# A linear-attention and feed-forward kernel: the opening's instructions in another order

## The chip, the cores and the metric

The kernel runs on one core of a Trainium2 chip. A core has five engines with queues of their own: TensorE (PE in the profile; its weight loads are PEld), VectorE (DVE), ScalarE (ACT), GpSimd (POOL) and SyncE (SP), which here only issues transfers. Sixteen DMA engines move data between the chip's large memory and the on-chip buffers. Matrix products land in PSUM, eight banks of 128 partitions by 512 fp32 numbers.

The metric is the device time of one execution in microseconds (us). The kernel before takes 286.4 us, the median of three runs (285.63, 286.40 and 286.46).

## The reference, cut to what matters

```python
batch, n_heads, seq, head_dim = (8, 8, 576, 64)
def phi(x):
    return np.where(x > 0, x, np.exp(x) - 1.0) + 1.0
q_p, k_p = (phi(q), phi(k))
kv = np.einsum('bhsd,bhse->bhde', k_p, v)
z = np.sum(k_p, axis=2)
num = np.einsum('bhsd,bhde->bhse', q_p, kv)
den = np.einsum('bhsd,bhd->bhs', q_p, z)[..., None] + 1e-06
x = (num / den)            # then heads side by side: 4608 tokens x 512
h = x @ w_in               # 512 x 2048
g = h - np.tanh(h)
out = g @ w_out            # 2048 x 512
```

Inputs and output are fp32; the kernel multiplies in bf16. phi is computed as min(exp(x), max(x, 0) + 1).

## The kernel before, in words

**Stages.** The feed-forward part goes over nine chunks `c` of 512 tokens. In each, layer 1 makes 16 blocks `fi` of 128 hidden columns (four matmuls each, `l1mm`, L418; tanh on ScalarE and the difference on VectorE, `l1act` and `l1act2`), and layer 2 makes four output blocks (`l2mm`, L439). The attention of the next batches is written between these steps by hand: the lists `s1[fi]` and `s2[s]` hold what is issued after a step. TensorE is busy almost without a pause in them. The order of the instructions of each engine is the order in which they are written, and each waits by semaphore counts for what it needs.

**The opening** is what comes before layer 1 of chunk 0: the attention of batch 0 cannot hide behind anything. A batch has 576 tokens and eight heads; heads are taken in four pairs `p`, and the eight heads lie as two halves `i`, two `hg` and two `h`, so that a product over 64 tokens and 64 dimensions uses a quarter of TensorE, and four run as one quad (`quads`). With J = 9 token groups:

1. `load` (L88) brings q, k and v of batch 0 by halves, `load_wi` (L107) w_in by column ranges, then k of batch 1, two parts of w_out, q and v of batch 1 (L91). All go through POOL's queue, which casts fp32 to bf16, in the order written; a load also waits until the eighth load before it has landed.
2. `spin` (L506) multiplies zeros while nothing else is there: 18 matmuls, later 5 and 6.
3. phi of q's halves (Exp L131, max L132, min L133), nine transposes per half on TensorE (`a_qT_pe`, L161), each half copied from two PSUM banks (L165 on ScalarE, L167 on VectorE).
4. phi of k. The second half goes in two parts by `h` (L128 to L130).
5. `b0_z` sums phi(k) over tokens by a matmul with ones, for each half (L247); `b0_zc` masks the sums into `kz` (L251).
6. `b0_kv` multiplies phi(k) and v (L257), `b0_kz` copies the result to `kz` (L261), on VectorE for half 0 and on ScalarE for half 1.
7. `a_den` (L326, L330) makes the denominators in bank 4, VectorE takes the reciprocal (L339).
8. `b0_num` multiplies kv and q of a half (L267) into two banks, `b0_evac` (L287) copies both banks to `ns` by one ScalarE instruction.
9. `b0_spread` spreads the reciprocals to the layout of `num` by fp32 matmuls into banks 4 to 7 (L294), `b0_scale` multiplies (L298): four pairs in the order 0, 2, 1, 3, first for the first 256 tokens, then for the next 256. Pairs 0 and 2 belong to half 0, 1 and 3 to half 1.
10. The first four blocks of layer 1 in chunk 0 (L642) go by 256 tokens and by pair, as the scales come.

Before the change the order on TensorE in steps 5 to 9 is z(0), kv(0), z(1), den, num(0), kv(1), num(1), spread.

**Later places that the prediction names.** In layer 2 of chunk 0, after its eighth step (`s2[7]`), TensorE transposes q of batch 1 (`a_qT_pe`, L161) and multiplies phi(k) and v of batch 1 (`a_kv`, L179). phi of that q is issued at `s2[3]` and `s2[4]` (L131 to L133).

## Time and profile before

| | |
|---|---|
| median of three runs | 286.4 us (285.63 to 286.46) |
| profiled execution | 286.08 us, its span 284.3 us |
| PE busy | 274.7 us, 97% of the span |
| DVE, ACT, POOL busy | 175.7, 146.2, 74.2 us |
| layer 1 matmuls (L418) | 121.8 us |
| layer 2 matmuls (L439) | 122.7 us |
| first matmul of layer 1, chunk 0 (L642) | begins at 16.66 us |
| instruction packets on queue q8 | 16, 0.26 MB |

The span is the time from the first to the last instruction of the profiled execution; its own time is 1.8 us longer. In a line of the timeline the first number is the start, the second the time covered, both in us; then the engine, the line of the kernel, what is written and read with its shape, how many instructions were merged, and in brackets how long the engine was idle before and what ended that. "issue" there means that the profile shows nothing that it waited for. In the chain that ended last each line is a piece of the last chain: start, length, what. A busy PE is not PE at its peak, since the ends of matmuls are modelled. An idle engine off that chain costs nothing. A load has landed when each of the sixteen DMA engines has set its completion mark; the trace has the time of each mark. A few matmul records are missing from a trace.

### The profile page before, as it was taken

Reading aid. Unit: us, or ns where it says so; the run is one execution under the profiler, and the core shown is the slowest. Engines: PE = TensorE matmul, PEld = TensorE weight load, DVE = VectorE, ACT = ScalarE, POOL = GpSimd, SP = SyncE. Lnnn points to the kernel's source line nnn. Section 1 sums busy time; section 2 is a strip of 40 time slices with the busy share of each in tenths; the row PEclk is TensorE's granted clock in tenths of the full one; section 3 lists DMA queues with packets and bytes.
Section 4 is the critical chain, followed back from the end, with each engine's and each line's share of the span. In section 5 each row is a group of like instructions: output and inputs, shape, how many; then the busy total and the mean of one; then the engine's idle time right before and its main releaser. Section 6 shows DMA issues by size and latency. Waiting matters only on the chain.

```text
span 284.3 us, 5076 instructions
## 1 busy us (share of the span) xinstructions
PE 274.7 (97%) x2071; PEld 131.7 (46%) x2099; DVE 175.7 (62%) x278; ACT 146.2 (51%) x178; POOL 74.2 (26%) x66
## 2 busy tenths in 40 slices
PE   8879999999999999999999999999999999999995
PEld 3564464444544454445444544454444444444443
DVE  5849977997479773976397638764770167006600
ACT  4638657847345663666355736672651365125411
POOL 8642030030260536143605360506050000000000
PEclk9999999999999999999999999999999999999999
DMA  6999999998992299038913692241115210230032
GB/s 105 187 206 213 207 206 207 232 167 158 230 234 67 58 198 220 8 85 141 222 36 77 102 233 74 48 108 41 36 24 116 59 34 2 59 80 10 2 74 74
DMA packets 38215, 32.99 MB, mean 116 GB/s; under 512 B 16016, under 2 KB 33840, under 8 KB 38064
## 3 DMA queue, kind: packets, MB, share of 16 engines
q0 software_dynamic: 17488, 18.35, 39.9%
q1 hardware_dynamic: 20544, 14.18, 20.0%
q8 instruction: 16, 0.26, 0.3%
q10 hardware_dynamic: 160, 0.13, 0.1%
q14 instruction: 7, 0.06, 0.1%
HBM read 38.01 MB, written 9.46 MB: 167 GB/s over the span
## 4 chain that ended last, share of the span: by engine, by line
PE 84%; DMA 11%; POOL 2%; issue 1%; DVE 0%; POOLq 0%
PE ps_all L439 40%; PE ps_all L418 39%; DMA v<-in_v_dram 8%; DMA w_in_sb<-in_moe_w_in_dram 3%; PE ps_all L179 2%; PE ps_all L267 1%; PE ps_all L676 1%; POOL v L88 0%; POOL kraw L88 0%; POOL qraw L88 0%; POOL v L473 0%; PE ps_all L275 0%; POOL qraw L91 0%; PE ps_all L330 0%; PE ps_all L161 0%
## 5 line engine op out<-in xcount | busy, mean ns | idle before, releaser
L439 PE MATMUL ps_all<-w_out_sb,gT 128*128 128x512 bf16 x543 | 122.7, 379 | 1.4 <-issue 0.8
L418 PE MATMUL ps_all<-xT,w_in_sb 128*128 128x512 bf16 x549 | 121.8, 379 | 0.7 <-issue 0.2
L425 DVE TENSOR_TENSOR gT<-ps_all,th 128x1024 bf16<-128x1024 f32 x64 | 77.8, 1218 | 47.0 <-ACT th L424 47.0
L424 ACT ACTIVATE th<-ps_all 128x1024 f32<-128x1024 f32 x64 | 65.6, 1024 | 47.7 <-PE ps_all L418 47.0
L418 PEld LDWEIGHTS <-w_in_sb 128*128 128x128 bf16 x560 | 54.6, 98 | 65.6
L439 PEld LDWEIGHTS <-gT 128*128 128x128 bf16 x560 | 53.8, 98 | 63.2 <-issue 0.2
L448 ACT COPY osb<-ps_all 128x512 f32<-128x512 f32 (+1 forms) x36 | 20.9, 583 | 56.6 <-PE ps_all L439 45.3
L238 POOL TENSOR_TENSOR qp<-qp,rd 128x1152 bf16<-128x1152 bf16 x10 | 21.0, 2119 | 39.1 <-issue 23.7
L224 POOL TENSOR_TENSOR pr<-qp,zb 128x1152 f32<-128x1152 bf16 x10 | 23.5, 2363 | 23.9 <-ACT zb L217 21.6
L131 ACT ACTIVATE e<-qraw 128x1152 bf16<-128x1152 bf16 x16 | 18.5, 1161 | 8.3 <-DMA qraw<-in_q_dram 8.3
L229 DVE TENSOR_REDUCE dn<-pr 128x9 f32<-128x576 f32 x20 | 14.5, 746 | 12.2 <-POOL pr L224 12.2
L131 ACT ACTIVATE e<-kraw 128x1152 bf16<-128x1152 bf16 x15 | 17.4, 1161 | 0.0
L133 DVE TENSOR_TENSOR qp<-e,r 128x1152 bf16<-128x1152 bf16 x16 | 12.1, 758 | 5.4 <-ACT e L131 4.5
L133 DVE TENSOR_TENSOR kp<-e,r 128x1152 bf16<-128x1152 bf16 x15 | 11.4, 759 | 5.2 <-ACT e L131 4.2
L91 POOL DMA_DIRECT2D kraw<-in_k_dram x7 | 5.6, 804 | 28.2 <-ACT e L131 19.8
L430 DVE TENSOR_TENSOR gT<-ps_all,th 128x512 bf16<-128x512 f32 x16 | 10.3, 686 | 3.1 <-ACT th L429 2.4
L429 ACT ACTIVATE th<-ps_all 128x512 f32<-128x512 f32 x16 | 9.2, 598 | 5.6 <-PE ps_all L642 4.4
L91 POOL DMA_DIRECT2D qraw<-in_q_dram x7 | 5.2, 744 | 23.3 <-DVE r L132 12.8
L378 DVE CAST xT<-ps_all 128x1024 bf16<-128x1024 f32 x5 | 6.1, 1217 | 6.9 <-PE ps_all L275 6.9
L506 PE MATMUL ps_all<-zero 128*128 128x512 bf16 x29 | 8.7, 460 | 1.2 <-DVE zero L460 1.2
L132 DVE TENSOR_SCALAR r<-qraw 128x1152 bf16<-128x1152 bf16 x16 | 7.5, 468 | 0.4 <-DMA qraw<-in_q_dram 0.4
L446 DVE COPY osb<-ps_all 128x128 f32<-128x128 f32 x1 | 0.3, 293 | 11.6 <-PE ps_all L676 11.6
(97 smaller groups left out, 137.8 us busy)
## 6 DMA issues: line engine op xcount, KB each, us to landing
out_dram<-osb SPq DMA_DIRECT2D x66, 128.0 KB, 2.3
kraw<-in_k_dram POOLq DMA_DIRECT2D x7, 576.0 KB, 6.6
qraw<-in_q_dram POOLq DMA_DIRECT2D x7, 576.0 KB, 8.5
v<-in_v_dram POOLq DMA_DIRECT2D x7, 576.0 KB, 11.8
w_in_sb<-in_moe_w_in_dram POOLq DMA_DIRECT2D x3, 512.0 KB, 13.2
w_out_sb<-in_moe_w_out_dram POOLq DMA_DIRECT2D x3, 512.0 KB, 18.7
rdb<-ds SPq DMA_DIRECT2D x2, 576.0 KB, 7.8
qraw<-in_q_dram POOLq DMA_DIRECT2D x2, 288.0 KB, 4.4
```

Of the source, the lines that this page charges most:

```text
L91: nc.gpsimd.dma_start(out=t.rearrange("q h i j d -> q (h i) (j d)"), in_=x.rearrange("(n q) x -> q n x", n=4))
L131: return (lambda: nc.scalar.activation(e, x, AF.Exp), lambda: nc.vector.tensor_scalar(r, x, 0.0, 1.0, ALU.max, ALU.add), lambda: nc.vector ...
L133: lambda: nc.vector.tensor_tensor(y, e, r, ALU.min))
L224: nc.gpsimd.tensor_mul(pr_t[b][:, i].rearrange("p j h d -> p j (h d)"), qp_t[b][:, i].rearrange("p j h d -> p j (h d)"), zb_t[b][:, i].uns ...
L229: nc.vector.tensor_reduce(dn_t[b][:, i, :, h], pr_t[b][:, i, :, h, :], mybir.AxisListType.X, ALU.add)
L238: nc.gpsimd.tensor_mul(x, x, rd[:, i].unsqueeze(2).to_broadcast([128, J * 2, D]))
L418: nc.tensor.matmul(h, w_in_sb[:, p, fi * 128:(fi + 1) * 128], xT[:, p, c * 512:(c + 1) * 512], start=(n == 0), stop=(n == NP - 1))
L424: nc.scalar.activation(th, h, AF.Tanh)
L425: nc.vector.tensor_sub(gT[:, fi:fi + 2, :], h, th)
L430: nc.vector.tensor_sub(gT[:, fi, :], h, th)
L439: nc.tensor.matmul(o, gT[:, fi, i * 128:(i + 1) * 128], w_out_sb[:, fi, :], start=(fi == 0), stop=(fi == NF - 1))
L448: nc.scalar.copy(osb[:, f0:f1], o[:, f0:f1])
```

## The change

The opening's instructions are rearranged; what is computed stays the same.

- Ninety-six tiny matmuls of zeros (24 quads of 64x64 weights and 2 columns) are issued first, and the spins after them fall from 18 to 14.
- The first half of k, the copies of the second transposed q half, and the second half of k are issued in another order; the last copy goes to VectorE instead of ScalarE. k's second half is now cut by token groups (the first six, the last three) instead of by `h`.
- z of half 0 is made with a two-column operand `two` that separates the two `hg`, nine matmuls of 128 rows in place of 18 of 64. Both z, both masks and the denominators come before kv(0).
- kv(1) comes before num(0), and the spread before num(1). The copy of `kz` for half 0 goes to ScalarE.
- `b0_evac` copies bank by bank; one bank of half 0 is copied by VectorE.
- The scales take pairs 0 and 2 for both token ranges first, then pairs 1 and 3. The first four blocks of layer 1 follow that by a written order.
- w_in's first 512 columns come in two loads of all 512 columns and half of the rows each (row blocks 0 and 2, then 1 and 3), instead of two loads of 256 columns and all rows.

```diff
         if parts:
 
-            return ([lambda h=h: nc.scalar.activation(e[:, h], x[:, h], AF.Exp) for h in range(2)],
+            js = [slice(0, parts), slice(parts, J)]
+            return ([lambda a=a: nc.scalar.activation(e[:, :, a], x[:, :, a], AF.Exp) for a in js],
                     lambda: nc.vector.tensor_scalar(r, x, 0.0, 1.0, ALU.max, ALU.add),
-                    [lambda h=h: nc.vector.tensor_tensor(y[:, h], e[:, h], r[:, h], ALU.min) for h in range(2)])
+                    [lambda a=a: nc.vector.tensor_tensor(y[:, :, a], e[:, :, a], r[:, :, a], ALU.min) for a in js])
...
-    def b0_z(i):
-
+    def b0_z0():
+
+        for j in range(J):
+            nc.tensor.matmul(ps_all[:, 5, 0:2], kp_t[0][:, 0, j].rearrange("p h d -> p (h d)"), two,
+                             start=(j == 0), stop=(j == J - 1))
+
+    def b0_z1():
         for j in range(J):
             for hg in range(2):
                 r = slice(64 * hg, 64 * hg + 64)
-                nc.tensor.matmul(ps_all[:, 4 - 2 * i + hg, 0:32], kp_t[0][r, i, j].rearrange("p h d -> p (h d)"),
+                nc.tensor.matmul(ps_all[:, 2 + hg, 0:32], kp_t[0][r, 1, j].rearrange("p h d -> p (h d)"),
                                  one[r, 0:32], start=(j == 0), stop=(j == J - 1))
 
-    def b0_zc(i):
-        nc.vector.tensor_mul(kz_t[0][:, :, i, 64:96], ps_all[:, 4 - 2 * i:6 - 2 * i, 0:32], mask[:, :, i, :])
+    def b0_zc():
+        for i, z in enumerate((ps_all[:, 5, 0:2].unsqueeze(2).to_broadcast([128, 2, 32]), ps_all[:, 2:4, 0:32])):
+            nc.vector.tensor_mul(kz_t[0][:, :, i, 64:96], z, mask[:, :, i, :])
...
     def b0_kz(i):
-        (nc.scalar.copy if i else nc.vector.tensor_copy)(kz_t[0][:, :, i, 0:64], ps_all[:, 2 * i:2 * i + 2, 0:64])
+        nc.scalar.copy(kz_t[0][:, :, i, 0:64], ps_all[:, 2 * i:2 * i + 2, 0:64])
...
-        b0 = 2 * i
-        nc.scalar.copy(ns[:, i::2, 0:8, :].rearrange("p a j t -> p a (j t)"), ps_all[:, b0:b0 + 2, :])
+        for h in range(2):
+            (nc.scalar.copy if i or h == 0 else nc.vector.tensor_copy)(
+                ns[:, 2 * h + i, 0:8, :].rearrange("p j t -> p (j t)"), ps_all[:, 2 * i + h, :])
...
-    for f0, n in ((0, 256), (256, 256), (512, 512), (1024, 512), (1536, 512)):
-        load_wi(f0, n)
+    for p in range(2):
+        nc.gpsimd.dma_start(out=w_in_sb[:, p::2, 0:512],
+                            in_=moe_w_in[:, 0:512].rearrange("(t p) f -> p t f", p=128)[:, p::2])
+    for f0 in (512, 1024, 1536):
+        load_wi(f0, 512)
...
+    nc.vector.memset(two, 0.0)
+    for hg in range(2):
+        nc.vector.memset(two[64 * hg:64 * hg + 64, hg:hg + 1], 1.0)
...
-    spin(18)
+    for _ in range(24):
+        for rs, cs, r, c in quads():
+            nc.tensor.matmul(ps_all[cs, r, 0:2], zero[rs, 0:64], zero[rs, 0:2], start=True, stop=True)
+    spin(14)
     a_qT_pe(0, 0, side, "AV")
-    (ek0, rk0, mk0), (ek1, rk1, mk1) = (phi_pieces(0, k_t, kp_t, "kp", i, 2 * i) for i in range(2))
-    for f in (ek0, rk0, *ek1, mk0, rk1):
+    (ek0, rk0, mk0), (ek1, rk1, mk1) = (phi_pieces(0, k_t, kp_t, "kp", i, 6 * i) for i in range(2))
+    for f in (ek0, rk0):
         f()
     spin(5)
-    a_qT_pe(0, 1, side, "AA")
+    a_qT_pe(0, 1, side, "AV")
+    for f in (*ek1, mk0, rk1, *mk1):
+        f()
     spin(6)
-    b0_z(0)
-    for f in mk1:
-        f()
-    b0_zc(0)
+    b0_z0()
+    b0_z1()
+    b0_zc()
+    a_den(0, 4)
     b0_kv(0)
-    b0_z(1)
-    b0_zc(1)
     b0_kz(0)
-    a_den(0, 4)
     ns0 = new_ns(0)
     b0_rest()
-    b0_num(0)
     b0_kv(1)
     b0_kz(1)
+    b0_num(0)
     b0_evac(0, ns0)
+    b0_spread((0, 2, 1, 3), 0)
     b0_num(1)
     b0_evac(1, ns0)
-    b0_spread((0, 2, 1, 3), 0)
-    for x in range(2):
-        for n, p in enumerate((0, 2, 1, 3)):
-            b0_scale(p, ns0, n, 4 * x, 4 * x + 4)
+    for n in (0, 2):
+        for x in range(2):
+            for m in range(2):
+                b0_scale(n // 2 + 2 * m, ns0, n + m, 4 * x, 4 * x + 4)
...
-            for x in range(2):
+            order = [((0, 1), 0, 0), ((0, 1), 2, 0), ((2,), 0, 0), ((2,), 2, 0), ((0, 1, 2), 0, 1), ((0, 1, 2), 2, 1),
+                     *[((3,), p, x) for x in range(2) for p in (0, 2)],
+                     *[(range(4), p, x) for x in range(2) for p in (1, 3)]]
+            for fis, p, x in order:
                 xs = slice(256 * x, 256 * x + 256)
-                for n, p in enumerate((0, 2, 1, 3)):
-                    for fi in range(4):
-                        nc.tensor.matmul(hs[fi][:, xs], w_in_sb[:, p, fi * 128:(fi + 1) * 128], xT[:, p, xs],
-                                         start=(x == 0 and n == 0), stop=(x == 1 and n == 3))
+                for fi in fis:
+                    nc.tensor.matmul(hs[fi][:, xs], w_in_sb[:, p, fi * 128:(fi + 1) * 128], xT[:, p, xs],
+                                     start=(p == 0 and x == 0), stop=(p == 3 and x == 1))
```

More of the change, by code (lines that the diff above doesn't have):

```diff
@@ L69 @@
     zero = const.tile([128, 512], BF16, name="zero")
+    two = const.tile([128, 2], BF16, name="two")
     one = const.tile([128, J * 16], BF16, name="one")
```

## The prediction

> **What bounds the kernel now.** I read the chain that ended last first. From 38.89 us to the end it is TensorE work with pauses of 0.01 to 0.16 us, so whatever the opening gains must still be there at 38.89, and there the chain hangs on loads, not on the opening:
>
> ```profile
> 6.24 8.54 DMA w_in_sb<-in_moe_w_in_dram
> ...
> 15.05 0.75 POOL qraw L91
> 15.80 1.07 POOL v L473
> 16.87 0.01 POOL vp L474
> 16.88 21.96 DMA v<-in_v_dram
> 38.85 0.04 issue
> 38.89 1.20 PE ps_all L179 x72
> ```
>
> The reader is to see that batch 1's v, issued at 16.88, landed at 38.85, and that its kv product (L179) began 0.04 us later. Next I read the timeline around that place:
>
> ```profile
> 31.22 7.07 PE L439 MATMUL ps_all<-w_out_sb,gT 128*128 128x512 bf16 x31
> ...
> 36.03 2.22 ACT L131 ACTIVATE e<-qraw 128x1152 bf16<-128x1152 bf16 x2 [2.96 <-DMA qraw<-in_q_dram]
> ...
> 38.03 0.58 PEld L161 LDWEIGHTS <-qp 128*128 128x128 bf16 x9 [0.24 <-DVE qp L133]
> 38.13 0.67 PE L161 MATMUL ps_all<-ident,qp 128*128 128x128 bf16 x9
> ...
> 38.89 1.04 PEld L179 LDWEIGHTS <-kp 64*64 64x64 bf16 x72 [0.27 <-DMA v<-in_v_dram]
> ```
>
> Batch 1's q landed at 36.00 and its Exp began at once; the transposes could start at 38.03, and TensorE came to them at 38.1. It then waited 0.27 us for v. So TensorE alone would have been 0.22 to 0.27 us earlier here: that is all that a faster opening can give while the loads land as they do. Stretches of 1 us show DMA at 196 to 240 GB/s from 15 us to 39 us, a full queue.
>
> Then the opening's timeline:
>
> ```profile
> 10.69 1.26 ACT L128 ACTIVATE e<-kraw 128x576 bf16<-128x576 bf16 x2 [1.01 <-DMA kraw<-in_k_dram]
> ...
> 11.41 1.03 DVE L130 TENSOR_TENSOR kp<-e,r 128x576 bf16<-128x576 bf16 x2 [0.32 <-ACT e L128]
> ...
> 13.57 1.06 DVE L339 RECIPROCAL rden<-ps_all 128x144 f32<-128x144 f32 x1 [0.22 <-PE ps_all L330]
> ...
> 14.87 1.17 PE L294 MATMUL ps_all<-rden,sel 32*128 32x128 f32 x32
> ...
> 16.18 2.74 DVE L298 TENSOR_TENSOR xT<-ns,ps_all 128x256 bf16<-128x256 f32 x8 [1.55 <-PE ps_all L294]
> 16.66 1.03 PE L642 MATMUL ps_all<-xT,w_in_sb 128*128 128x256 bf16 x8 [0.61 <-DVE xT L298]
> ...
> 18.25 2.50 PEld L642 LDWEIGHTS <-w_in_sb 128*128 128x128 bf16 x23 [0.73 <-issue]
> ```
>
> The path is k's second half, phi, z, den, reciprocal, spread, scale, first layer. The last line is odd: TensorE stood still from 17.53 to 18.25 although the scale it needed had ended at 17.27 and w_in's second load had its last completion mark at 16.14. The DMA view of 15.9 to 17 us holds the only candidate:
>
> ```profile
> q8 instruction: 1, 0.02, 5.5%
> ```
>
> One 16 KB packet of instructions began at 15.97. The page counts 16 such packets, and the program has some 4,160 TensorE instructions, about 260 to a packet. The weight load that stopped is TensorE's 402nd; L294's sixteen fp32 matmuls come before it, and if each is eight instructions (a fit; the trace shows four) it is the 514th, two blocks' end. My reading, an inference: TensorE ran out of instructions.
>
> **The change, part by part** (before → after, us in the profiled execution).
>
> *Tiny matmuls for four spins.* A cold spin takes 0.427 (starts of L506 until 5.0), a warm one 0.216; four cold ones are 1.7. The 24 tiny quads are not in the trace. The nearest rows are the 64x64 quads of L257, 0.0315 a quad warm; cold, doubled as the spins are, 24 take 1.5. Bounds: 0.76 warm; 2.4 if each pair costs what a pair of L247 does (0.025), doubled. I take 1.5: the first transposes wait for qp until 7.38 and the spins ended at 7.04, so it costs nothing; at 2.4 about 0.5 would show, inside the later cover.
>
> What they move is the instruction count: +184 here, +166 by the first layer. The next refill packets after TensorE was released at 38.89 and 45.28 began at 42.16 and 48.55, 3.3 later each, so the one of 15.97 was called for at about 12.7, which is where TensorE passed instruction 256; its content was in use 5.6 later. After the change instruction 256 follows the second transposes' first weight load (the 252nd), released when qp ends at 8.88. So new instructions come at u = 8.9 + 5.6 = 14.5, and they are needed from about the 513th, which is now in kv(1), just before num(0) and the spread.
>
> [...]
>
> *k's second half in two token groups; the copies.* Exp: 0.67 for 576 and 1.16 for 1152 columns give 0.83 for 768; it starts at 10.69 as before. DVE now copies part of the second qT (0.42, L167) before kp's first half: 9.76 to 10.18, min to 10.96, r to 11.42, then mins of 0.56 and 0.36: ends 12.40 (before 12.44). ACT's two late copies (1.16 at 11.86) fall to one, in its idle second before 10.69: free. z: the first half's nine matmuls stand under the mins; after 12.40 six matmuls are left rather than 18: kz's masks end 12.95 (13.16), reciprocal 13.36 to 14.42 (13.57 to 14.63): 0.21 gained.
>
> *kz(0) by ScalarE, kv(0) after den.* 0.27 on ACT (L261's row) at about 13.6, ahead of nothing; kv(0) starts 13.1 rather than 12.06. It hides under the reciprocal's 1.06 as far as instructions allow: kv(1) ends and num(0) begins at u = 14.5. Spread 14.75 (14.87), after it num(1).
>
> *Evacuation and scales.* DVE takes one bank of num(0): between its 256-column row (0.41) and its 1024-column cast (1.22) about 0.68, 15.0 to 15.7, before the spread ends: free. The first scale still waits for the whole spread: 16.06 (16.18). num(1) is now behind the spread; its two bank copies on ACT (1.02 a pair, L287) end 17.25, before the pairs 1 and 3 that need them at 17.39 and 17.72, because those scales now come fifth.
>
> *First layer's new order and no stop.* Scales every 0.331, matmuls every 0.109: start 16.53, fi 0 and 1 wait 0.11 once, end 20.14 (20.86). The added waits of fi 2 and 3 for ACT's copies of banks 2 and 3 (16.7 and 17.25) end before their turns (17.08 and 17.96); behind them would stand the rest of the first layer. So the opening is 0.72 shorter; 0.6 of it is the stop.
>
> *w_in by rows.* 512-byte packets become 1,024-byte ones. v's second half was complete at 13.41, both w_in loads at 16.14: 2.73 for 0.52 MB; w_in's columns 1024 to 1535, as much data in 1,024-byte packets, 2.53 (marks at 19.12 and 21.65). So 0.2 off everything queued behind. Bounds: 0 and 0.2. POOL's issue rows (0.75 each, five as before) do not move.
>
> *At 38.89.* TensorE comes to the transposes at 37.4, q's phi lets them start at 37.9, v lands at 38.65: L179 starts at 38.7. The sum is **-0.2**, all of it from the packets: 286.08 - 0.2 = 285.9. The profiled execution stands 0.3 under the median 286.4 of three runs (285.63 to 286.46), so I put the median at 286.0. The difference that a measurement of this kernel tells from none is about 0.3%, 0.86 us.
>
> **The rivals.**
>
> *B, the loads come earlier too.* The sixteen marks of v's landing lie between 37.05 and 38.85, the median at 37.3: one DMA engine is 1.5 late. Its lag grew from 0.9 to 1.7 between 21.65 and 24.99, around the refill packet of 21.91 (1.0 long) and an 8 KB one at 20.55. After the change the refills come at about 12.2, 17.8 and 27; if none meets the slow engine, v is up to 0.8 earlier, and with 0.2 the shortened opening counts: 0.72 + 0.22 = 0.94 off, 285.1; with no instruction wait at all 1.05, 285.0. Against it: a third refill now falls before v.
>
> *C, slower: the missing instructions now stand on the path.* In before the stop lay in the first layer; now it lies before the spread, and behind num(0) and the spread wait every scale and the whole first layer. The end is 286.08 - 0.94 + (u - 14.5) once that passes -0.2: nothing is lost until u = 15.4, 0.3% at 16.3, and at u = 18.2, the clock time of the refill in before, +2.8 (288.9). For it: 5.6 is one reading, and the call for instructions was inferred. Against: 42.16 and 48.55 agree on its first 3.3.
>
> *D, the clock stays slow.* Spins fell from 0.427 to 0.216 at 5.2, 3.9 after the first. If tiny matmuls do not raise the clock and all 14 spins are cold, they end at 2.7 + 6.0 = 8.7, 1.2 after qp: the DVE chain above shifts by 1.15, the opening is 0.43 longer than before, +0.2 (286.3); with tinies at 2.4 another 0.9, +1.1. Against it: the tinies themselves keep TensorE issuing.
>
> [...]
>
> **How the numbers follow.** Likeliest A (loads decide): 0.45. B: 0.30. C beyond 0.3%: 0.20. D: 0.05, counted as no change. A's own range is 285.5 to 286.7 (the runs' spread around it). To hold 8 in 10 the range takes in B (285.0, less 0.1 for the spread) and C up to +1.1, leaving out its rest, about 0.15: 284.9 to 287.2. Faster 0.30, same 0.50, slower 0.20.
>
> **What would show it.** The stop before the 18.25 line gone; a `q8` packet near 12.2; the first scale near 16.06 and the last 256-column matmul near 20.1; L161 waiting 0.4 or more for qp, and v's landing directly before L179 at 38.7. Wrong if L179 starts before 38.2 (B), or if num(0) or the spread starts after 15.4 with idle time that nothing releases (C).

## The result, and the profile after

The changed kernel takes 286.38 us (median of 22 executions, 286.04 to 287.45); the kernel before took 286.08 beside it (22 executions, 285.62 to 286.46). The medians differ by 0.30 us. The ratio over all executions is 1.0019, 95% interval 1.0012 to 1.0025, which is 0.34 to 0.72 us longer. That is under the 0.3% that the prediction called the limit of a measurement here; 22 executions of each resolve it all the same. The time lies in the predicted range (284.9 to 287.2), and "no change" was the likeliest case, but the forecast itself was -0.2 us, and the sign is the other one.

The profiled execution took 286.37 us (before 286.08). Its span is 284.47 us (284.29), so 1.90 us lie around it instead of 1.79. In the opening's timeline (columns as before: start, time covered, engine, line, what, idle time and its releaser in brackets) these lines answer to those of the prediction (the changed kernel's line numbers are higher: its L163 is L161 before the change, L181 is L179, L427 is L418, L457 is L448):

```profile
1.19 1.45 PE L530 MATMUL ps_all<-zero 64*64 64x2 bf16 x96 [1.19 <-DVE zero L469]
...
6.68 2.29 ACT L133 ACTIVATE e<-qraw 128x1152 bf16<-128x1152 bf16 x2 [4.44 <-DMA qraw<-in_q_dram]
...
8.69 0.68 PE L163 MATMUL ps_all<-ident,qp 128*128 128x128 bf16 x9 [1.27 <-DVE qp L135]
...
14.36 1.06 DVE L348 RECIPROCAL rden<-ps_all 128x144 f32<-128x144 f32 x1 [0.42 <-PE ps_all L339]
...
15.47 1.17 PE L303 MATMUL ps_all<-rden,sel 32*128 32x128 f32 x32
...
16.78 2.74 DVE L307 TENSOR_TENSOR xT<-ns,ps_all 128x256 bf16<-128x256 f32 x8 [0.44 <-PE ps_all L303]
...
17.25 3.77 PE L662 MATMUL ps_all<-xT,w_in_sb 128*128 128x256 bf16 x32 [0.27 <-DVE xT L307]
...
20.75 10.14 PEld L427 LDWEIGHTS <-w_in_sb 128*128 128x128 bf16 x48
```

The tiny matmuls take 1.45 us (1.5 was estimated), and the stop of 0.7 us in the first layer is gone: the 32 matmuls of L662 run through. But Exp of q begins at 6.68 instead of 5.43, and everything behind it is late: the reciprocal at 14.36 (13.57), the first scale at 16.78 (16.18). TensorE comes to the next blocks of layer 1 (L427) at 20.75; in the kernel before, the first weight load of the same place (L418) stands at 20.75 too, and layer 2 starts at 31.22 in both. What the new order and the missing stop gain was lost at the start.

Why q is late stands in the DMA view of 4.5 to 5.6 us:

```profile
q0 software_dynamic: 199, 0.21, 113.8%
q8 instruction: 1, 0.02, 5.5%
```

The first 16 KB instruction packet now comes at 4.60 us and takes 0.96 us, while q's first half is landing. Fifteen of that load's sixteen marks are set by 5.41; the last is set at 6.66 (5.40 before). The page counts 17 packets instead of 16.

Then the place where the loads of batch 1 meet layer 2, and the chain that ended last from there on (start, length, what):

```profile
38.12 0.67 PE L163 MATMUL ps_all<-ident,qp 128*128 128x128 bf16 x9
...
38.81 1.04 PEld L181 LDWEIGHTS <-kp 64*64 64x64 bf16 x72 [0.20 <-DMA v<-in_v_dram]
```

```profile
38.82 8.16 DMA qraw<-in_q_dram
46.97 0.02 issue
46.99 0.02 ACTq L133
47.01 0.36 issue
47.38 1.16 ACT e L133
48.54 0.47 ACT osb L457
49.01 0.90 ACT e L133
49.91 0.07 issue
49.98 0.57 ACT osb L457
50.55 1.06 ACT e L133
51.61 0.48 ACT osb L457
52.10 0.04 issue
52.14 6.20 PE ps_all L427 x28
```

v again lands just before its product (38.77, L181 at 38.82; before 38.85 and 38.89). The chain, however, no longer runs over TensorE from there. It goes over ScalarE: batch 2's q has its last mark at 46.97, its Exp begins only at 47.38, 0.41 later (0.09 later in the kernel before: mark 46.79, Exp 46.88), and behind it in ScalarE's order stand the output copies (L457) that free TensorE's banks; TensorE waits 0.3 us at 52.1. The second kv product of the chunk loop (L181) starts at 58.27, 19.46 us after the first; before it was 19.16. So the span's 0.18 us is this 0.30, less 0.07 gained at 38.8, less 0.04 further on (the rest is rounding). This is the account of one execution: the profiled ones of a0, a19, a16 and after_cols (below) have the same late Exp, and there the second product follows after 19.20 or 19.21 us, since batch 2's q landed 7.91 or 7.92 us after L181 began and not 8.16. In a16_less it landed 8.81 after, and the second product followed after 20.10. What the late Exp costs thus depends on where that load lands.

### The profile page after: what moved, and what is told of

Read it like the earlier page. It is cut to its first block, busy times and chain, and to the rows that moved or that the text cites. A ratio compares the mean times of both kernels' runs of the same rounds, so it can differ in the third digit from the quotient of the medians.

```text
span 284.5 us, 5277 instructions
## 1 busy us (share of the span) xinstructions
PE 277.4 (98%) x2182; PEld 132.6 (47%) x2182; DVE 176.6 (62%) x282; ACT 145.6 (51%) x179; POOL 74.0 (26%) x66
## 4 chain that ended last, share of the span: by engine, by line
PE 77%; DMA 16%; ACT 3%; POOL 2%; issue 1%; DVE 1%; SPq 0%; POOLq 0%; ACTq 0%
PE ps_all L427 38%; PE ps_all L448 35%; DMA qraw<-in_q_dram 10%; DMA w_in_sb<-in_moe_w_in_dram 3%; DMA out_dram<-osb 2%; ACT e L133 2%; PE ps_all L181 1%; PE ps_all L275 1%; ACT osb L457 1%; POOL v L89 0%; SPq L464 0%; POOL kraw L89 0%; POOL qraw L89 0%; DVE qp L135 0%; PE ps_all L216 0%
## 5 line engine op out<-in xcount | busy, mean ns | idle before, releaser
L448 PE MATMUL ps_all<-w_out_sb,gT 128*128 128x512 bf16 x560 | 124.6, 379 | 0.0
L427 PE MATMUL ps_all<-xT,w_in_sb 128*128 128x512 bf16 x560 | 122.8, 379 | 0.1
L427 PEld LDWEIGHTS <-w_in_sb 128*128 128x128 bf16 x560 | 54.6, 98 | 65.9 <-issue 0.4
L448 PEld LDWEIGHTS <-gT 128*128 128x128 bf16 x560 | 53.8, 98 | 63.3 <-issue 0.2
L457 ACT COPY osb<-ps_all 128x512 f32<-128x512 f32 (+1 forms) x36 | 20.8, 582 | 56.6 <-PE ps_all L448 40.3
L231 DVE TENSOR_REDUCE dn<-pr 128x9 f32<-128x576 f32 x20 | 14.5, 745 | 12.2 <-POOL pr L226 12.2
L521 PE MATMUL ps_all<-zero 128*128 128x512 bf16 x25 | 7.5, 458 | 0.0
```

What stands on the lines that cost most here:

```text
L231: nc.vector.tensor_reduce(dn_t[b][:, i, :, h], pr_t[b][:, i, :, h, :], mybir.AxisListType.X, ALU.add)
L427: nc.tensor.matmul(h, w_in_sb[:, p, fi * 128:(fi + 1) * 128], xT[:, p, c * 512:(c + 1) * 512], start=(n == 0), stop=(n == NP - 1))
L448: nc.tensor.matmul(o, gT[:, fi, i * 128:(i + 1) * 128], w_out_sb[:, fi, :], start=(fi == 0), stop=(fi == NF - 1))
L457: nc.scalar.copy(osb[:, f0:f1], o[:, f0:f1])
```

## The experiments

The runs were made in groups, each with 23 to 35 executions of the kernel before beside it: 285.9 to 286.0 us, span 284.1 to 284.2, 1.77 us around the span. Eleven or twelve executions of each kernel were timed (22 of the change). The table has the medians; the ratio is over all executions and can differ from that of the medians; "around" is the mean of time less span (its standard error is 0.01 to 0.02).

| kernel | time, us | ratio to before, 95% | span | around |
|---|---|---|---|---|
| the change | 286.38 | 1.0019 (1.0012 to 1.0025) | 284.45 | 1.94 |
| a0 | 286.22 | 1.0013 (1.0004 to 1.0023) | 284.30 | 1.93 |
| a19 | 286.34 | 1.0024 (1.0011 to 1.0038) | 284.45 | 1.91 |
| a16 | 286.23 | 1.0012 (1.0001 to 1.0023) | 284.25 | 1.95 |
| b24 | 286.10 | 1.0010 (0.9999 to 1.0022) | 284.30 | 1.78 |
| bw | 286.17 | 1.0009 (0.9998 to 1.0020) | 284.40 | 1.78 |
| after_cols | 286.21 | 1.0012 (1.0002 to 1.0022) | 284.30 | 1.91 |
| after_pad | 286.62 | 1.0022 (1.0011 to 1.0033) | 284.50 | 2.10 |
| a16_cols_pad | 285.93 | 1.0006 (0.9992 to 1.0021) | 283.80 | 2.11 |
| before_less | 285.91 | 0.9999 (0.9983 to 1.0014) | 284.10 | 1.78 |
| a16_less | 286.31 | 1.0020 (1.0011 to 1.0029) | 284.35 | 1.96 |
| before_shift | 286.23 | 1.0011 (1.0001 to 1.0021) | 284.50 | 1.77 |
| a16_shift | 286.18 | 1.0012 (0.9998 to 1.0026) | 284.10 | 2.13 |
| after_cols_pad | 286.57 | 1.0018 (1.0003 to 1.0033) | 284.45 | 2.12 |
| order_only | 286.16 | 1.0002 (0.9986 to 1.0018) | 284.05 | 2.10 |
| before_noload | 285.90 | 0.9994 (0.9978 to 1.0010) | 284.10 | 1.77 |
| a16_noload | 285.84 | 0.9995 (0.9972 to 1.0017) | 283.70 | 2.12 |
| a16_cols_join | 285.89 | 1.0007 (0.9994 to 1.0021) | 284.15 | 1.80 |
| before_act3 | 286.47 | 1.0020 (1.0012 to 1.0029) | 284.40 | 2.10 |

The medians of the span have 95% intervals of some 0.3 us to either side, in some rows more; a difference of 0.2 between two rows is not resolved by itself. The last column is sharp.

### 1. Where the instruction packets fall (a0, a19, a16, b24)

**a0**: the changed kernel without the tiny matmuls.

```diff
-    for _ in range(24):
-        for rs, cs, r, c in quads():
-            nc.tensor.matmul(ps_all[cs, r, 0:2], zero[rs, 0:64], zero[rs, 0:2], start=True, stop=True)
-    spin(14)
+    spin(18)
```

> The changed kernel without the 96 tiny matmuls, 18 spins as before. Theory R (TensorE's first instruction refill is called at about its 193rd instruction, begins 3.3 us after that, occupies one DMA engine for 1 us and makes the load then running land about 1 us late): the first 16 KB instruction packet moves from 4.6 to 16 (+-0.7) us, q's first half lands at 5.4 rather than 6.7, the first transposes start at 7.4 rather than 8.7, and the stop of 0.7 to 1.0 us returns to the first layer; the 512-column matmuls of layer 1 start at 20.6 to 21.0, batch 1's v lands at 38.7. Time 286.0 to 286.2, that is 0.2 to 0.4 under the changed kernel and level with the kernel before. Rival S (q's late landing has another cause, and the count of instructions means nothing): q still lands near 6.7, no stop, time as the changed kernel, 286.4.

Measured: the first packet is back at 16.9 us, q's last mark at 5.51, Exp of q at 5.53. Rival S expected q to stay near 6.7, and is excluded. The stop is back too, in the chain of this kernel:

```profile
16.44 2.13 PE ps_all L659 x17
18.57 0.69 issue
19.27 1.80 PE ps_all L659 x15
```

Over the traces the stop goes with the packet: in the eight kernels whose first packet comes at 15.3 to 16.9 us, TensorE stops in the first layer for 0.4 to 0.9 us, and each stop ends 2.25 to 2.47 us after that packet began. The other twelve have no such stop.

**a19** and **a16**: 19 and 16 tiny quads instead of 24 (`range(19)`, `range(16)`).

> 19 tiny quads instead of 24, 14 spins. R: the 193rd instruction is now one of the first transposes, which wait for q until 7.4, so the packet begins near 10.7, after q and k have landed; q's first half lands at 5.4, no stop in the first layer, the 512-column matmuls of layer 1 start at 19.6 to 19.9, one us earlier than in either kernel. If the loads of batch 1 bound the end (theory A of the prediction), TensorE then waits 0.6 us or more for q and v of batch 1, its kv product starts at 38.6 to 38.8 all the same and the time is 285.8 to 286.0. If the loads do not bound it (theory B), that product starts before 38.2 and the time is 285.1 to 285.4. Rival S: as the changed kernel, 286.4.

> 16 tiny quads, 14 spins. R: the 193rd instruction comes after the second transposes' first weight load, released near 8.9, so the packet begins near 12.2 and q lands at 5.4; the instructions from about the 450th on (in kv(1)) are usable only near 14.5, so TensorE may stop there for up to 1 us; the 512-column matmuls start at 19.8 to 20.6. Time by the loads 285.8 to 286.1. Rival S: as the changed kernel, 286.4.

Measured: with 19 quads the packet still comes at 4.70 and q's last mark at 6.81, so a19 missed: if a count of instructions calls for the packet, it is a lower one than I took from the trace. With 16 quads it comes at 11.81, q lands at 5.42, and there is no stop in the first layer. In its place a wait stands ahead of kv(1), and so ahead of the spread:

```profile
13.21 1.06 DVE L348 RECIPROCAL rden<-ps_all 128x144 f32<-128x144 f32 x1 [0.42 <-PE ps_all L339]
...
14.40 0.48 PE L265 MATMUL ps_all<-v,kp 64*64 64x64 bf16 x36 [0.84 <-DMA v<-in_v_dram]
...
15.03 0.98 PEld L303 LDWEIGHTS ps_all<-rden,sel 32*128 32x128 f32 x32 [0.23 <-issue]
...
16.81 3.77 PE L662 MATMUL ps_all<-xT,w_in_sb 128*128 128x256 bf16 x32 [0.27 <-DVE xT L307]
```

The reciprocal ends at 14.27 and the spread starts at 15.03, 0.76 later (0.05 in the changed kernel). What is late is a load again: v's second half has fifteen of its sixteen marks by 13.14 and the last at 14.36, kv(1) starts 0.04 later (L265, 14.40), and num(0) and the spread stand behind it. The packet of 11.81 thus does to v what that of 4.60 does to q. So it is in five of the six kernels with 16 quads (last mark 0.85 to 1.32 after the fifteenth); in a16_cols_join it is not (0.02). Even so layer 2 of chunk 0 starts at 30.77 rather than 31.22, so the opening is 0.45 us shorter. L181 starts at 38.94, 0.04 after v's last mark: the 0.45 is gone at the load, and the time is no better.

**b24**: the kernel before with the 24 tiny quads and 14 spins, nothing else.

> The kernel before with the 24 tiny quads and 14 spins alone. R: packet at 4.6, q's first half lands at 6.6, the first transposes start at 8.7 (7.44 before), the stop of 0.7 in the first layer goes; the 512-column matmuls of layer 1 start at 21.2 to 21.5 (20.9), batch 1's kv product at 39.0 to 39.4 (38.89); time 286.2 to 286.6. Rival S: as the kernel before but without the stop, 285.9 to 286.1, or no difference.

Measured: packet at 4.5, q's last mark at 6.84, first transposes at 8.88, no stop. Layer 2 of chunk 0 starts at 31.30 (31.22 in the kernel before). Batch 1's kv product at 38.80 and the time of 286.10 lie just under what was expected. This line of its timeline answers to the Exp of q at 6.68 above (5.43 in the kernel before):

```profile
6.87 2.33 ACT L131 ACTIVATE e<-qraw 128x1152 bf16<-128x1152 bf16 x2 [4.63 <-DMA qraw<-in_q_dram]
```

One edit to the old kernel thus makes both effects. Its span is longer by 0.35 us in the mean (interval 0.08 to 0.65). What follows: the tiny matmuls move the instruction packet (4.5 us instead of 15.97), and the packet costs about as much at q as its absence gains later. That part is shown.

### 2. w_in by rows, and ScalarE's place in its program (bw, after_cols, after_pad, a16_cols_pad)

**bw**: the kernel before with only w_in's first loads by rows.

```diff
-    for f0, n in ((0, 256), (256, 256), (512, 512), (1024, 512), (1536, 512)):
-        load_wi(f0, n)
+    for p in range(2):
+        nc.gpsimd.dma_start(out=w_in_sb[:, p::2, 0:512],
+                            in_=moe_w_in[:, 0:512].rearrange("(t p) f -> p t f", p=128)[:, p::2])
+    for f0 in (512, 1024, 1536):
+        load_wi(f0, 512)
```

> The kernel before with w_in's first 512 columns by rows, nothing else changed. Theory W (the row loads are slower on the queue, 3.15 us for the pair instead of 2.7, and that is what the changed kernel loses): the pair's median marks stand 3.1 to 3.2 apart from v's second half, batch 1's v ends 0.2 to 0.45 later than 38.85, L179 starts at 39.1 to 39.3 and the time grows by 0.2 to 0.45 us. Theory S (the loss is ScalarE's late Exp of batch 2's q in chunk 1): the pair is 0.45 longer too, but the last mark of batch 1's v is set by the slowest of the sixteen DMA engines and stays within 0.1, Exp of batch 2's q starts 0.1 after its load's last mark as in the kernel before, and the time stays within 0.1 us of the kernel before.

**after_cols**: the changed kernel with that edit undone.

> The changed kernel with w_in's first 512 columns in two loads of 256 columns again. W: the pair takes 2.7 us again and the 0.3 us are gone, time equal to the kernel before within 0.1 us. S: the pair takes 2.7 us again, but Exp of batch 2's q still starts 0.4 us after its load's last mark and the time stays 0.2 to 0.4 us above the kernel before.

Measured, from v's second half to the second w_in load by the median of the sixteen marks: 2.71 us before, 2.70 in after_cols, 3.17 in bw, 3.13 in the changed kernel. The rows are 0.45 us slower on the queue, all of it in the first of the two loads (1.85 instead of 1.35 in bw). In time bw is 0.2 us longer (its span by 0.21 in the mean, 0.01 to 0.43), and v's last mark lies at 39.02; undoing it in the changed kernel leaves 286.21. So the loss on the queue is shown, and over all twenty kernels the pair takes 2.92 to 3.20 us by rows and 2.65 to 2.82 by columns; its price in time, between 0 and 0.4 us, is not resolved. ScalarE's late Exp is as it was in after_cols (0.41 after the mark), and on time in bw (0.08).

**after_pad**: the changed kernel with one more one-column Exp at the very start.

```diff
     nc.scalar.activation(act0, zero[:, 0:1], AF.Exp)
+    nc.scalar.activation(act0, zero[:, 0:1], AF.Exp)
```

> The changed kernel with one more one-column Exp on ScalarE at the very start, so that every later ScalarE instruction is one further in its stream, as in the kernel before. S: Exp of batch 2's q starts 0.05 to 0.15 us after its load's last mark instead of 0.41, the pause of TensorE at 52.1 shrinks by 0.3 and the time is equal to the kernel before within 0.1 us. W: nothing moves, the time stays 0.2 to 0.4 us above the kernel before.

One premise of that text was wrong. In ScalarE's written program the wait for batch 2's q and its Exp are instructions 62 and 63 before the change, and 64 and 65 after it: later, not one earlier; the pad makes them 65 and 66. Its effect came as expected:

```profile
47.79 1.16 ACT L133 ACTIVATE e<-qraw 128x1152 bf16<-128x1152 bf16 x1 [1.90 <-DMA qraw<-in_q_dram]
```

The mark is at 47.71, so Exp is 0.08 behind it, and the second kv product starts 19.15 after the first again. In this execution v itself was late (last mark 39.76), hence the later clock times. The delay is 0.39 to 0.41 in all six kernels that have wait and Exp at 64 and 65 (the change, a0, a19, a16, after_cols, a16_less), and 0.08 or 0.09 in the other fourteen. The time, however, became longer: 286.62. Time less span shows why: 2.10 us instead of 1.94.

**a16_cols_pad**: 16 quads, w_in by columns and the pad together.

> The changed kernel with 16 tiny quads instead of 24 (the first instruction packet then leaves q's load alone and the opening is 0.45 us shorter), w_in by columns, and the extra ScalarE instruction. S and W together: both losses are gone, the time is that of the kernel before or up to 0.2 us less. Theory L (loads decide at L179): L179 starts at 38.8 to 38.95 although the opening ends 0.45 us earlier, so the gain is no more than 0.2 us. If the loads do not decide, L179 starts at 38.4 to 38.5 and the time falls by 0.4 us.

Measured: a span of 283.8, 0.4 us under the kernel before (interval of the difference -0.75 to +0.10), the shortest but one of all; with 2.11 us around it the time is 285.93, equal to before. The profiled execution was its longest (287.22), and its page shows why, in the TensorE clock that was granted in 40 equal slices of the span (tenths of full speed):

```profile
PEclk9979999999999999999999999999999999999999
```

The clock was halved from 14.55 to 17.96 us, when the spread and the first scales run; the spread takes 2.09 us instead of 1.17, and layer 2 of chunk 0 starts at 32.25. The mean granted clock of this execution is 0.992. Such executions (0.988 to 0.994, where all others have 0.997 to 1.000) are 12 of the 60 of a16_cols_pad, a16_shift, order_only, a16_noload and a16_cols_join, 4 of the 105 of the other kernels with the new order, 3 of the 163 of the kernel before in these groups and none of the 70 of its variants. Why the new order has more of them was not tested.

### 3. Do the loads decide? (before_less, a16_less, before_shift, a16_shift, before_noload, a16_noload)

**before_less** and **a16_less** load w_out's second quarter last; chunk 0 multiplies by the first quarter in its place.

```diff
-    load_wo(1)
...
     load_wo(3)
+    load_wo(1)
...
+            elif c == 0 and g == 1:
+                for fi in range(4, 8):
+                    nc.tensor.matmul(os_[i], gT[:, fi, i * 128:(i + 1) * 128], w_out_sb[:, fi - 4, :],
+                                     start=False, stop=False)
```

> The kernel before with 0.5 MB less ahead of batch 1's q and v on the queue: the second quarter of w_out is loaded last of the first loads, and layer 2 of chunk 0 multiplies its second quarter of gT by the first quarter of w_out instead (this part of chunk 0's output is thus not the reference's; its matmuls cost the same). Theory L (the loads of q and v of batch 1 set the time at L179): q and v land 2.5 us earlier, TensorE no longer waits for them, L179 starts 0.2 to 0.3 us earlier, at about 38.6, and the whole is 0.2 to 0.3 us shorter. If TensorE alone sets the time, nothing moves.

> The changed kernel with 16 tiny quads, and with the second quarter of w_out loaded last as in before_less (chunk 0's second quarter of layer 2 again uses the first quarter of w_out). Theory L: with the loads out of the way the opening that is 0.45 us shorter counts in full: L179 starts at 38.1 to 38.2 and the time is 0.4 to 0.5 us under before_less, 0.6 to 0.8 under the kernel before. If the gain of the opening is lost elsewhere than at the loads, the time stays within 0.15 us of before_less.

Measured: in both the wait for v is gone, and L179 (L181) starts at 38.21 and 38.14. The time of before_less is that of the kernel before (0.9999), so theory L missed its 0.2 to 0.3. Its profiled execution is 0.67 us shorter, but its layer 2 already starts 0.51 us earlier, because k's second half happened to land at 10.05 instead of 10.60. a16_less, expected 0.4 to 0.5 under before_less, is 0.40 above it, and shows where a gain at 38.1 goes:

```profile
47.34 1.16 ACT L133 ACTIVATE e<-qraw 128x1152 bf16<-128x1152 bf16 x1 [3.11 <-DMA qraw<-in_q_dram]
...
52.10 2.10 PE L427 MATMUL ps_all<-xT,w_in_sb 128*128 128x512 bf16 x8 [0.52 <-ACT osb L457]
```

Batch 2's q, whose place on the queue did not move, lands at 46.95, its Exp comes 0.39 later, and TensorE waits for the output copies behind it. The second kv product starts at 58.24, as in the changed kernel. So a second load sits 8 us behind the first.

**before_shift** and **a16_shift** move the load of v of batch 1 between the two loads of w_out's third quarter, and its product one step of layer 2 later; the second spread goes from step 12 to 13. a16_shift is a16_cols_pad with that edit.

```diff
-            s2[7].append(lambda: (a_qT_pe(1, 0, Banks([4, 5])), a_kv(1, 6), a_qT_pe(1, 1, Banks([4, 5]))))
-            s2[8].append(lambda: (scale_rest(0, 6, rdb_t[0]), a_den(1, 4), num1(), a_split(1)))
-            s2[10].append(lambda: spread1(0))
+            s2[7].append(lambda: a_qT_pe(1, 0, Banks([4, 5])))
+            s2[8].append(lambda: (a_qT_pe(1, 1, Banks([4, 5])), a_kv(1, 6)))
+            s2[9].append(lambda: (scale_rest(0, 6, rdb_t[0]), a_den(1, 4), num1(), a_split(1)))
+            s2[11].append(lambda: spread1(0))
```

> The kernel before with w_out's first half of the third quarter loaded ahead of batch 1's v, and that batch's second transposes and kv one step of layer 2 later, its denominators and spreads one step later too. Theory L: v lands at about 40.1 when TensorE comes for it at 40.3, the wait for v is gone and the time falls by up to 0.25 us. Rival: the wait moves to the spread of batch 1's reciprocals or to the scales ahead of chunk 1, and the time is equal or up to 0.5 us longer.

> The changed kernel with 16 tiny quads, w_in by columns, the extra ScalarE instruction, and the later place of batch 1's v as in before_shift. Theory L: the shorter opening now counts, 0.4 to 0.45 us under before_shift and 0.4 to 0.7 under the kernel before. If the wait only moves to the spread or the scales it is equal to before_shift less 0.4.

Measured: 1.0011 and 1.0012, no gain; the spans are 284.5 and 284.1. That is the rival's case, also in that a16_shift's span is before_shift's less 0.4.

**before_noload** and **a16_noload** never load w_out's second quarter, so that batch 2's q is early too.

```diff
-    load_wo(1)
...
-            nc.tensor.matmul(o, gT[:, fi, i * 128:(i + 1) * 128], w_out_sb[:, fi, :],
+            nc.tensor.matmul(o, gT[:, fi, i * 128:(i + 1) * 128], w_out_sb[:, fi - 4 if fi // 4 == 1 else fi, :],
```

> The kernel before without the load of w_out's second quarter: layer 2 uses the first quarter of w_out in its place in all chunks, at the same cost of matmuls (the output is thus not the reference's). All loads behind it come 2.5 us earlier, batch 2's q too. Loads decide: L179 at 38.2 to 38.6, Exp of batch 2's q before 45.5, and the time 0.3 to 0.7 us under the kernel before. If the loads don't decide, no change.

> The changed kernel with 16 tiny quads, w_in by columns and the extra ScalarE instruction, and again without the load of w_out's second quarter (the first is used in its place). Loads decide: with none of them in the way the shorter opening shows at the end, L179 at 37.8 to 38.2 and the time 0.3 to 0.5 us under before_noload. If the new opening gives nothing of its own, the time equals before_noload within 0.15 us.

Measured: before_noload does not move (span 284.10, difference 0.00, -0.30 to +0.30): 2.5 us less of queue gives the kernel before nothing that can be seen. a16_noload has a span of 283.70, 0.40 under before_noload as expected, though with a wide interval (-1.05 to +0.55 against the kernel before), and its time is only 0.06 shorter; a16_cols_pad, with all its loads, has 283.80. Much of that width goes with the granted clock: it was low in 4 of a16_noload's 12 executions and in 2 of a16_cols_pad's. In the mean of the span, the other eight of a16_noload lie 0.71 us under before_noload (interval 0.36 to 1.03) and 0.40 under the other ten of a16_cols_pad (0.06 to 0.72). That choice was made after the fact, so it is a hint and not a test. So "the loads decide" is true of single executions, in which the last mark and the start of L179 lie 0.04 us apart; it is not what holds the median of the kernel before, and whether it holds back the new opening stays open.

### 4. The rest of the loss (after_cols_pad, order_only, a16_cols_join, before_act3)

**after_cols_pad** undoes both losses of part 2 in the changed kernel; **order_only** drops the tiny matmuls as well (as in a0).

> The changed kernel with both undone: w_in by columns and the extra ScalarE instruction; the 24 tiny quads, the early refill and the new order stay. If the row loads and ScalarE's late Exp are all of the loss, the time is that of the kernel before within 0.1 us. If the third refill ahead of batch 1's loads (three packets instead of two before 30 us) is the cause, it stays 0.2 to 0.4 us above, with a last mark of batch 2's q later than 46.8 us.

> The changed kernel without the tiny quads (18 spins as before), with w_in by columns and the extra ScalarE instruction: the new order of the opening alone, with two refills before 30 us as in the kernel before. All theories of the loss (row loads, ScalarE, third refill) expect the time of the kernel before within 0.1 us, since q and v of batch 1 and q of batch 2 land as before. If the order itself costs, the time is 0.2 us or more above.

Measured: after_cols_pad 286.57, not equal to before: its span is 0.35 us above (0.05 to 0.45), with q's last mark at 7.08. order_only has a span equal to before's (284.05; -0.40 to +0.35), and its time is 0.24 longer by what lies around it. In its profiled execution the chain runs over batch 2's k (landed at 50.16), and the second kv product follows 19.56 after the first: a third load behind the second. The kernels with the early packet (the change, a19, b24, after_cols, after_pad, after_cols_pad) have spans of 284.30 to 284.50; those with the new order, columns and Exp on time but no early packet (a16_cols_pad, a16_shift, order_only, a16_noload, a16_cols_join) 283.70 to 284.15; those without the early packet but with rows and the late Exp (a0, a16, a16_less) 284.25 to 284.35. That a third packet falls ahead of the loads would be a cause common to the second group too (a16_cols_pad has three before 32 us); that it falls into q's load is what sets the first group apart. The plainest pair is after_cols_pad and a16_cols_pad, which differ in eight tiny quads alone: 0.65 in the median of the span, 0.45 in the mean (0.12 to 0.74).

**a16_cols_join** keeps 16 quads and columns and joins two of ScalarE's copies; **before_act3** adds three one-column Exps to the kernel before.

```diff
+        if i:
+            nc.scalar.copy(ns[:, i::2, 0:8, :].rearrange("p a j t -> p a (j t)"), ps_all[:, 2:4, :])
+            return
```

```diff
     nc.scalar.activation(act0, zero[:, 0:1], AF.Exp)
+    nc.scalar.activation(act0, zero[:, 0:1], AF.Exp)
+    nc.scalar.activation(act0, zero[:, 0:1], AF.Exp)
+    nc.scalar.activation(act0, zero[:, 0:1], AF.Exp)
```

> The changed kernel with 16 tiny quads, w_in by columns, and num's second half copied by one ScalarE instruction for both banks, as in the kernel before; no extra ScalarE instruction. ScalarE's program has 311 instructions (310 before, 312 after, 313 with the extra one). Theory P (the time outside the span follows ScalarE's instruction count: 1.77 us at 310, 1.94 at 312, 2.11 at 313): 1.80 to 1.90 us outside the span. Exp of batch 2's q, now the 64th instruction instead of the 65th, starts 0.05 to 0.15 after its load's last mark. Span median 283.8 as in a16_cols_pad, time 285.6 to 285.7, 0.2 to 0.4 under the kernel before. If the time outside the span belongs to the new opening in general (VectorE's five more instructions, say), 1.94 and a time of 285.75 or more.

> The kernel before with three more one-column Exps on ScalarE at the very start, so that its program has 313 instructions like that of after_pad; they run while the first load is on its way. P: 2.05 to 2.15 us outside the span instead of 1.77, the span the same within 0.15, the time 0.3 longer than before. If the count of ScalarE's instructions has nothing to do with it: 1.77 outside, time the same within 0.1.

Measured: before_act3 has 2.10 us around its span where the kernel before has 1.77, and takes 286.47 (1.0020). The three Exps run from 2.27 to 2.93, while ScalarE waits for q until 5.47:

```profile
2.27 0.20 ACT L463 ACTIVATE act<-zero 128x1 f32<-128x1 bf16 x1
...
2.50 0.20 ACT L464 ACTIVATE act<-zero 128x1 f32<-128x1 bf16 x1
...
2.73 0.20 ACT L465 ACTIVATE act<-zero 128x1 f32<-128x1 bf16 x1
```

So theory P is shown for the time around the span. Over all twenty kernels it goes with the number of instructions in ScalarE's written program and with nothing else that was varied: 1.77 to 1.78 at 310, 1.80 at 311, 1.91 to 1.96 at 312, 2.10 to 2.13 at 313. The span of before_act3 is 0.2 to 0.3 longer too, which P did not expect; why is open. a16_cols_join has its 1.80 and Exp 0.08 after the mark, but a span of 284.15, not 283.8 (3 of its 12 executions had the low clock; the median of the others is 284.0); its time is that of the kernel before. No kernel here beats the kernel before by more than its interval.

## Why the prediction was wrong

**The size.** 286.38 less 286.08 is 0.30 us; by the ratio it is 0.34 to 0.72. Of this 0.17 lies around the span (1.94 less 1.77). The rest is in it: 0.13 by the medians of the first measurement, 0.25 to 0.35 when the span of 284.45 is put beside the 284.1 to 284.2 of the kernel before in the later groups. The sum of the prediction was made for the span alone and took what lies around it as constant.

**The tiny matmuls "cost nothing".** Their own time was right (1.45), they end under the wait for qp, and rival D did not happen in the profiled execution: the clock rose at 5.96 (a spin takes 0.216 us from there on and 0.427 before), and the spins ended at 7.42. Wrong was what they move. The step "instruction 256 follows the second transposes' first weight load ... u = 8.9 + 5.6 = 14.5" failed: the packet came at 4.60, not 12.2. The fit of instruction counts (eight to an fp32 matmul, a call at the 256th) was made to one stop, and no other run shows it: 16 quads or 19 decide between 11.8 and 4.7. Whether a count of instructions calls for the packet, and which, stays open. No rival had the packet collide with q's load, though B and C both argued from packets that delay something. (In B's row it is not one DMA engine alone that is late: v's last two marks are at 38.24 and 38.85, 0.9 and 1.5 after the median.) That the stop would vanish was right.

**The opening "0.72 shorter".** In the changed kernel it is 0.00 shorter (the next blocks' first weight load at 20.75 in both). Without the collision at q it is 0.45 (a16), with 0.76 lost ahead of the spread to the packet's collision with v's second half. Rival C, missing instructions there, did not happen in either: in the changed kernel the spread starts 0.05 after the reciprocal, in a16 the wait ends with v's last mark. The spread, the first scale and the next blocks' first matmul came 0.72 after the forecast times (15.47, 16.78 and 20.86 for 14.75, 16.06 and 20.14), the reciprocal 1.00 after its own, so the working between them held; what went wrong is q's 1.25 at its head.

**"At 38.89 ... the loads decide".** The place and the order were right: transposes, v's landing, L181 at 38.82; but TensorE came to the transposes at 38.12, not at 37.4. The step was short by one load: in the profiled execution batch 2's q decides again at 47 us. And with the loads taken away the median of the kernel before does not move, so the 0.22 to 0.27 us, "all that a faster opening can give while the loads land as they do", was read from one execution.

**"-0.2, all of it from the packets".** This term had the wrong sign. The pair takes 3.13 us instead of 2.71, not 2.53; the bounds "0 and 0.2" excluded a loss with no reason, when the row used for it was a load of another shape.

**Not in the sum at all:** ScalarE's program is two instructions longer (a copy and a wait, net of the copies added and dropped). The prediction priced its copies by whom they delay ("free", "ahead of nothing"). They lengthen what lies around the span by 0.17 us (before_act3 shows that the count alone does it) and move Exp of batch 2's q to the 65th place, where it starts 0.3 us late (shown by after_pad); with it the second product came 0.30 us later in this execution and 0.05 in four others. How the rest in the span divides between that Exp, the row loads and the early packet is not settled; a0 against order_only gives the first two 0.25 together, b24 gives the packet 0.2 to 0.35 and after_cols_pad against a16_cols_pad 0.45 to 0.65, with intervals about as wide as the values, and they do not add.

## What to carry to other kernels

An instruction cost more here than its duration on its engine: 24 tiny quads for four spins moved the first instruction packet from 15.97 us to 4.5 (b24), into q's load, and three more instructions on ScalarE lengthened the time around the span from 1.77 to 2.10 us (before_act3). So when a few tenths of a microsecond are at stake, count each engine's instructions and look in the trace which load a packet runs into. Never give a load of another shape a one-sided bound (2.53 us was expected of the row loads, 3.13 came). Before crediting a wait to "the load that lands last", look for the next load behind it (8 us behind it here), and compare several executions' spans and granted clocks, for one trace shows one draw of the landings.

## What the runs showed of the hardware that was not expected

- A 16 KB instruction packet took 0.96 us in the changed kernel, and the load that was landing at that time had its last mark late while the fifteen others were in time: q's first half by 1.22 to 1.57 us in the six kernels with the early packet (0.00 to 0.09 in the other fourteen), v's second half by 0.85 to 1.32 in five of the six with 16 quads. In the eight kernels whose first packet came at 15.3 to 16.9 us, TensorE stopped for 0.4 to 0.9 us in the first layer.
- The time around the span grew from 1.77 to 2.10 us with three more ScalarE instructions, none of which anything waited for. What happens in it the trace does not show.
- Exp started 0.39 to 0.41 us after its data's last mark when the wait ahead of it was the 64th instruction of ScalarE's program, and 0.08 to 0.09 with the wait at 62, 63 or 65. The reason was not tested.
- In the changed kernel's trace the clock rose at 5.96 us, 3.4 after the first full-size spin and 4.8 after the first tiny matmul. Over the eight kernels without tiny matmuls, whose spins all begin at 1.2, it rose 2.7 (a0) to 5.8 us (order_only) after the first spin, over the twelve with them 3.3 to 5.7, so these runs do not show whether tiny matmuls count.
- The clock was also halved once within an opening, from 14.55 to 17.96 us, and that execution's span was 285.1 us where the median of its kernel is 283.8.
- Half of w_in's rows in 1,024-byte packets took 1.85 us where half of its columns in 512-byte packets took 1.35; the second load of each pair took 1.32 and 1.36. The cause is open.
